# Four reorderings in a tuned convolution and SoLU kernel: transposes of y, one load of x, squares, and the last tiles' halves

## The chip, the core and the metric

The kernel runs on one core of a Trainium2 chip. The metric is the device time in microseconds (us) of one execution, from launch to end, as the median of several runs. A profile of one execution lies beside it; its span, from the first to the last instruction, is a little shorter than the time of that execution.

The engines of the core are named as the profile names them: PE (matrix multiplication; PEld is its weight load, which overlaps it), DVE, ACT and POOL (elementwise work), and SP, which here only issues transfers. Each engine works through its own list in order. All transfers of this kernel, plain ones and transposing ones, are issued by SP, one after the other, so a transfer whose data aren't ready holds up everything behind it in SP's list.

## The reference

Two layers, on x of 8 x 4160 x 192 and 33,280 tokens of 192 numbers after the first:

```python
# first: a causal convolution over 7 rows, one set of 7 softmaxed taps for each of 8 heads of 24 columns
x_unf = x_pad[:, idx, :].reshape(B, S, K, H, group)
out = np.einsum('hk,bskhg->bshg', w, x_unf)
# second: for each token
h = x @ w_in                                   # 192 -> 1024
e = np.exp(h - h_max)
solu = h * e / (np.sum(e) + 1e-09)
ln = (solu - mean) / np.sqrt(var + 1e-06) * g_ln
out = ln @ w_out                               # 1024 -> 192
```

The kernel keeps single precision by splitting numbers into a high and a low float16 half and multiplying the halves.

## The kernel before

**Chunks.** The 8 sequences are cut into 17 chunks: the first sequence into rows 0 to 1023, 1024 to 2079 and 2080 to 4159 (chunks 0, 1, 2), each of the others into two halves of 2080 rows (chunks 3 to 16). A chunk is worked in windows of 112 rows. Its x is loaded in pieces of five windows (`load`, lines 139 to 167, tile `xr`, eight buffers), scaled and split on POOL and ACT (`halve_steps`, lines 234 to 243, tile `xs`), convolved on PE group by group (`product`, line 281, result `pc` in a single PSUM bank), read out by ACT (`upper`, line 313) and DVE (`lower`, line 322) into `y16`, and transposed by SP into `yT` (`turn`, line 352). A chunk of 19 windows is turned in two parts, windows 0 to 9 and 10 to 18, each in three blocks of columns in the order 1, 0, 2. Half of block 1 is then copied to `y2` by a plain transfer (`double`, line 365). The largest value of a chunk's x, from which its scale follows, is taken by `sum_squares`: ACT squares (line 187) or DVE maxima (line 181).

**Tiles.** The second layer goes over 260 tiles of 128 tokens, numbered from 0. A tile's way is: eight matmuls of `emit_rows` (line 736, from `yT`) and two of `emit_third` (line 759) into a pair of PSUM banks `ph`; `emit_max` on DVE (line 790); `emit_exp` on ACT (797); `emit_mul` on DVE (807); `emit_hi` on ACT, the float16 upper half (815); `emit_lo` on POOL, the lower half (827), and at once its transpose into `pT` by SP (829); `emit_out` on PE, 16 or 24 matmuls (844) into a single bank `po`; `emit_evac` on DVE (854 or 852), which frees that bank. `emit_square` on ACT (819) only sums squares for the variance; its result is wanted at the end of a group of up to eight tiles, when `Group.roots` runs on POOL (912 to 916) and the rows are scaled (`row`, 921 and 925) and stored (934).

There are three pairs of banks for `ph`, so tile k+3's first matmul waits for tile k's `emit_mul`. There are two single banks, used in turn by everything that needs one: each `po`, each `pc`, the pieces of `split_taps`. The third use waits until the first has been read out.

**Order.** The schedule is written out by hand: the order of the calls in the source is the order in each engine's list. `three_steps(i)` (line 1279) emits one step of three tiles a, b, c = i, i+1, i+2, for i = 8, 11, 14 and so on. In a step PE does `emit_out` of tile i-5, the rows of a, then b, `emit_out` of i-4, the rows of c, `emit_out` of i-3, with up to four groups of convolution at the places 0 to 3 between them. `chores` (line 968) assigns to each tile of a chunk what is to be done for the chunks ahead: groups to convolve, pieces to load, to sum, to open, to turn, to double. Steps 8, 11 and 14 are marked `start` (`PAIRED` is 8). In later steps, what `chores` has to turn is put into the list `moves` at the end of the step; `move()` takes one of them, at the end of the step and after the lower halves of a and of b in the next one. The last step, tiles 257, 258 and 259, is `last_three` (line 1468).

The program below is printed with the lines of the profile.

Of the kernel before, what the change touches and what calls it, by code (L numbers as in the profile page):

```python
# [8 lines left out]
F16 = mybir.dt.float16  # L9
# [4 lines left out]
ALU = mybir.AluOpType  # L14
# [5 lines left out]
def kernel(  # L20
# [9 lines left out]
    nc = tc.nc  # L30
    P = 128
# [5 lines left out]
    NFC = F // P  # L37
    NH = F // 512
# [4 lines left out]
    FIRST = 1024  # L43
# [743 lines left out]
    def emit_max(t):  # L787

        t.bias = sp.tile([P, 1], F32, name=f"sm_{t.i}", tag="sm", bufs=4)
        dve.tensor_scalar(  # L790
            t.ph, t.ph, t.cv[:, 0:1], None, ALU.mult, ALU.min, accum_out=t.bias
        )

    def emit_exp(t):
        g, grp = t.g, t.grp
        t.e = sp.tile([P, F], F32, name=f"e_{t.i}", tag="e", bufs=4)
        act.activation(  # L797
            t.e, t.ph, AF.Exp, bias=t.bias, scale=-1.0, accum_out=grp.z[:, g : g + 1]
        )
# [17 lines left out]
    def emit_square(t):  # L817
        junk = sp.tile([P, F], F32, name=f"sq_{t.i}", tag="sq", bufs=1)
        act.activation(  # L819
            junk, t.e, AF.Square, accum_out=t.grp.s2[:, t.g : t.g + 1]  # L820
        )
        if t.g == t.grp.n - 1 and t.g:
            t.grp.squares()
            queue.put(t.grp.steps(), first=True)

    def emit_lo(t, eng):
        eng.tensor_tensor(t.p16[:, :, 1, :], t.halves, t.p16[:, :, 0, :], ALU.subtract)  # L827
        t.pT = sp.tile([P, 2 * NFC, P], F16, name=f"pT_{t.i}", tag="pT", bufs=4)
        nc.sync.dma_start_transpose(t.pT, t.p16.rearrange("p n a f -> p (n a f)"))

    def emit_out(t):
        t.po = single(f"po_{t.i}")
        t.wide = t.grp.n > 1 and t.i >= PAIRED

        ops, per = [], NFC // NH
        for c in range(NFC):
            hi = c // per * 2 * per + c % per
            if t.wide:
                ops.append((hi, ohl[:, c].rearrange("p a d -> p (a d)"), 2 * D))
            else:  # L840
                ops += [(hi, ohi[:, c], D), (hi, olo[:, c], D)]
            ops.append((hi + per, ohi[:, c], D))
        for j, (a, w, n) in enumerate(ops):
            nc.tensor.matmul(  # L844
                t.po[:, 0:n], t.pT[:, a, :], w, start=j == 0, stop=j == len(ops) - 1
            )
# [231 lines left out]
    def run_stores():  # L1078
        while stores:
            stores.pop(0)()  # L1080
# [42 lines left out]
    def numerators(t):  # L1123
        emit_mul(t)
        emit_hi(t)
# [148 lines left out]

    def loads(work):
        for c, j in work.get("load", []):
            c.load(j)

    def three_steps(i):

# [17 lines left out]
        urgent = i == PAIRED + 3  # L1298

        start = i < 2 * PAIRED  # L1300
        if not start:
            loads(work)
        got = {}
# [33 lines left out]
        def move():  # L1337

            for f in moves[:1]:
                f()  # L1340
            del moves[:1]

        def openings():
            for k in work.get("open", []):
                k.open(lefts[k.ch], chunks[k.ch - 1])
            for k, piece in work.get("turn", []):
                k.turn(*piece)

        run_stores()
        emit_out(done[0])  # L1350

# [7 lines left out]
        if start:  # L1359
            emit_max(a)  # L1360
            emit_exp(a)
            if i == PAIRED:
                for k, h in late:
                    sum_up(k, h, i - 1)
        for q in squares:
            emit_square(q)
        squares.clear()
        add(0)
        if not start:
            emit_max(a)  # L1370
# [6 lines left out]
        lowers(1)  # L1377
        emit_exp(b)
        if start:
            second()  # L1380
            if i > PAIRED:
                for k, h in late:
                    sum_up(k, h, i - 1)
                late.clear()
                uppers(2)
            for k, q in doubles:
                k.double(*q)
            doubles.clear()
        numerators(a)
        emit_lo(a, pool)  # L1390
        move()
        if i == PAIRED:
            uppers(2)
            late[:] = after
        if urgent:
            openings()
        run_stores()
# [23 lines left out]
        for d in done[2:]:  # L1421
            emit_out(d)
        place(3)
        emit_max(c)
        uppers(3)
        emit_exp(c)
# [11 lines left out]
            add(1)  # L1438
        numerators(c)
        if at(3):  # L1440
            emit_square(b)
        if PAIRED < i < 2 * PAIRED:
            add(1)
        queue.run(3.8 if i < 20 else 2.0)
        emit_lo(c, pool)
        squares.append(c)
        if urgent:
            for k, q in work["double"]:
                k.double(*q)
        elif start:  # L1450
            openings()
            doubles.extend(work.get("double", []))
        else:
            for k in work.get("open", []):
                k.open(lefts[k.ch], chunks[k.ch - 1])
            moves.extend(lambda k=k, q=q: k.turn(*q) for k, q in work.get("turn", []))
            move()
            doubles.extend(work.get("double", []))
        if i == NT - 6:
# [4 lines left out]
    def ready(t):  # L1464
        emit_z(t)
        emit_root(t)

    def last_three(i):


        a, b, c = [prepare(i + j) for j in range(3)]
        done = tiles[i - DEPTH : i]
        assert all(t.grp.n == 1 for t in (*done[3:], a, b, c))
        run_stores()
        take_rooted()
        emit_a(a, b, c, lambda: emit_out(done[0]))
        for t in (b, c):
            emit_rows(t, False, True)
        for t in squares:
            emit_square(t)  # L1480
        emit_evac(done[0])
        emit_max(a)
        emit_exp(a)
        ready(done[4])
        emit_out(done[1])
        numerators(a)
        emit_lo(a, pool)
# [67 lines left out]
```

## Time and profile before

| | before |
|---|---|
| median of 3 runs | 1171.81 us (1171.79 to 1172.24) |
| the profiled execution | 1172.57 us, of which the span is 1170.9 us |
| mean granted clock of PE | 0.995 |
| busy share of the span | PE 97%, DVE 87%, ACT 85%, POOL 75% |
| matmuls | 7742 |
| the transfer queue of SP | 225.53 MB, 99.1% of 16 transfer engines' span |
| HBM | 33.00 MB read, 25.56 MB written |

How to read it: busy shares are means over the span. The profile's list of waits gives, for an engine and a line, what it waited for, in total, how often, and the longest. A row of the timeline gives the start in us from the span's start, the duration, the engine and line, what is written and read, the number of merged instructions, and in brackets the idle time before the first of them and what ended it. A row of the stretches gives the busy time of each engine in that stretch and, after POOL's, the granted clock of PE (1.00 is full speed).

### The profile page before, as it was taken

What the parts mean: (1) busy time and instruction counts of PE and PEld (TensorE: products, weight loads), DVE (VectorE), ACT (ScalarE), POOL (GpSimd) and SP (SyncE); (2) the same over time, 40 slices, a digit from 0 to 9 for tenths busy, and PEclk for the clock granted to TensorE, in tenths of its full rate; (3) what the DMA queues carried; (4) which work ended last, traced back from release to release, by engine and by line L of the source; (5) the groups of instructions that cost most, each with busy time, mean ns of one, the idle gap of its engine ahead of it and who ended that gap; (6) DMA issues with size and microseconds to landing.
All of it is one profiled execution on the core that took longest, in us unless ns stands there. A gap on an engine that the chain in (4) does not pass through costs nothing.

```text
span 1170.9 us, 22364 instructions
## 1 busy us (share of the span) xinstructions
PE 1137.6 (97%) x7742; PEld 695.9 (59%) x7742; DVE 1017.8 (87%) x2057; ACT 997.3 (85%) x1772; POOL 878.2 (75%) x684
## 2 busy tenths in 40 slices
PE   6899998999999999999999999999999999999997
PEld 3565555666565665655656666665665666566555
DVE  8888887988989898998889989888898998788786
ACT  6998887888888898888888888888888889888885
POOL 2746778988878688887868888688788868855564
PEclk9999999999999999999999999999999999999999
DMA  8799999999999999999999999999999998999978
GB/s 224 173 185 182 179 198 201 201 194 207 188 202 208 197 190 211 216 183 204 200 199 191 208 217 184 193 208 202 202 207 199 194 193 172 173 159 196 185 150 175
DMA packets 727295, 226.95 MB, mean 194 GB/s; under 512 B 651518, under 2 KB 725774, under 8 KB 727182
## 3 DMA queue, kind: packets, MB, share of 16 engines
q1 hardware_dynamic: 727182, 225.53, 99.1%
q8 instruction: 60, 0.98, 0.3%
q14 instruction: 53, 0.43, 0.1%
HBM read 33.00 MB, written 25.56 MB: 50 GB/s over the span
## 4 chain that ended last, share of the span: by engine, by line
PE 82%; POOL 4%; DVE 4%; issue 3%; DMA 3%; ACT 3%; SPq 0%; DVEq 0%; POOLq 0%; ACTq 0%
PE po L844 37%; PE ph L736 34%; PE pc L281 5%; PE ph L759 5%; POOL p L827 2%; DMA pT<-p 2%; DVE ph L790 1%; DVE e L807 1%; ACT e L797 1%; ACT p L815 1%; DMA yT<-y 1%; POOL xs L243 1%; DMA raw_in<-in_moe_w_in_dram 1%; POOL xr L240 1%; ACT sq L819 0%
## 5 line engine op out<-in xcount | busy, mean ns | idle before, releaser
L827 POOL TENSOR_TENSOR p<-e,p 128x1024 f16<-128x1024 f32 x259 | 552.4, 2137 | 234.7 <-ACT p L815 234.4
L844 PE MATMUL po<-ohl,pT 128*128 128x192 f16 (+1 forms) x4264 | 541.6, 284 | 8.8 <-DMA pT<-p 5.3
L844 PEld LDWEIGHTS <-pT 128*128 128x128 f16 x4264 | 385.7, 98 | 168.9 <-DMA pT<-p 7.6
L736 PE MATMUL ph<-whi,yT 128*128 128x512 f16 x1548 | 420.0, 380 | 8.2 <-DMA yT<-y 5.5
L790 DVE TENSOR_SCALAR_CACHE_REDUCE ph<-ph,cv 128x1024 f32<-128x1024 f32 x248 | 318.9, 1287 | 75.0 <-PE ph L759 58.3
L797 ACT ACTIVATE e<-ph,sm 128x1024 f32<-128x1024 f32 x260 | 289.2, 1112 | 101.3 <-DVE ph L790 95.1
L807 DVE SCALAR_TENSOR_TENSOR e<-ph,cv,e 128x1024 f32<-128x1024 f32 x248 | 316.9, 1278 | 22.4 <-ACT e L797 22.2
L736 PEld LDWEIGHTS <-yT 128*128 128x128 f16 x2064 | 192.6, 98 | 237.6 <-issue 36.4
L815 ACT CAST p<-e 128x1024 f16<-128x1024 f32 x260 | 269.9, 1039 | 32.7 <-DVE e L807 32.2
L819 ACT ACTIVATE sq<-e 128x1024 f32<-128x1024 f32 x260 | 273.5, 1052 | 0.1
L736 PE MATMUL ph<-wlo,yT 128*128 128x512 f16 x516 | 153.5, 379 | 0.0
L854 DVE TENSOR_REDUCE raw<-po 128x192 f32<-128x384 f32 x247 | 136.2, 551 | 15.9 <-PE po L844 15.6
L243 POOL TENSOR_TENSOR xs<-xr,xs 128x960 f16<-128x960 f32 (+1 forms) x56 | 107.7, 1922 | 1.4
L313 ACT ACTIVATE y<-pc 112x432 f16<-112x432 f32 (+5 forms) x140 | 62.7, 469 | 17.3 <-PE pc L281 8.6
L759 PE MATMUL ph<-wlo,yT 64*128 64x512 f16 x269 | 74.0, 380 | 0.0
L281 PE MATMUL pc<-xs,taps_hi 128*112 128x240 f16 (+1 forms) x448 | 73.0, 261 | 0.0
L322 DVE SCALAR_TENSOR_TENSOR y<-pc,y 112x432 f16<-112x432 f32 (+5 forms) x140 | 72.2, 532 | 0.7 <-ACT y L313 0.7
L759 PE MATMUL ph<-wlo,y 64*128 64x512 f16 x251 | 68.6, 380 | 0.0
L181 DVE TENSOR_REDUCE xa<-xr 128x1 f32<-128x384 f32 x112 | 66.5, 616 | 2.1 <-DMA xr<-in_x_dram 2.1
L281 PEld LDWEIGHTS <-taps_hi 128*112 128x112 f16 x448 | 52.4, 130 | 16.7 <-DVE xm L203 0.3
L240 POOL TENSOR_SCALAR xr<-xr,s 128x960 f32<-128x960 f32 (+1 forms) x56 | 57.4, 1026 | 3.0
L281 PE MATMUL pc<-xs,taps_lo 128*112 128x240 f16 (+1 forms) x224 | 58.5, 261 | 0.0
(146 smaller groups left out, 785.4 us busy)
## 6 DMA issues: line engine op xcount, KB each, us to landing
out_dram<-raw SPq DMA_DIRECT2D x127, 192.0 KB, 2.9
xr<-in_x_dram SPq DMA_DIRECT2D x41, 480.0 KB, 4.8
xr<-in_x_dram SPq DMA_DIRECT2D x22, 384.0 KB, 4.1
pT<-p SPq DMA_TRANSPOSE x260, 4.6
y<-yT SPq DMA_DIRECT2D x15, 140.0 KB, 3.1
y<-yT SPq DMA_DIRECT2D x15, 126.0 KB, 2.8
yT<-y SPq DMA_TRANSPOSE x102, 3.7
raw_out<-in_moe_w_out_dram SPq DMA_DIRECT2D x1, 1536.0 KB
```

The lines of the kernel that those rows point to most:

```text
L243: (2.1 * size + 0.2, lambda: pool.tensor_tensor(xl, r, h, ALU.subtract)),
L281: nc.tensor.matmul(o, tp[:, h + j, :], r, start=q == 0, stop=q == len(ops) - 1)
L736: nc.tensor.matmul(bank, lhs, w[:, r, n * 512 : (n + 1) * 512], start=start and j == 0, stop=stop and j == len(ops) - 1,)
L759: nc.tensor.matmul(banks_of(t)[n], y[q, t.off : t.off + P], wlo[q, 1, n * 512 : (n + 1) * 512], start=start, stop=not start,)
L790: dve.tensor_scalar(t.ph, t.ph, t.cv[:, 0:1], None, ALU.mult, ALU.min, accum_out=t.bias)
L797: act.activation(t.e, t.ph, AF.Exp, bias=t.bias, scale=-1.0, accum_out=grp.z[:, g : g + 1])
L807: dve.scalar_tensor_tensor(t.e, t.ph, t.cv[:, 3:4], t.e, ALU.mult, ALU.mult, accum_out=t.grp.s1[:, t.g : t.g + 1],)
L815: act.copy(t.p16[:, :, 0, :], t.halves)
L819: act.activation(junk, t.e, AF.Square, accum_out=t.grp.s2[:, t.g : t.g + 1])
L827: eng.tensor_tensor(t.p16[:, :, 1, :], t.halves, t.p16[:, :, 0, :], ALU.subtract)
L844: nc.tensor.matmul(t.po[:, 0:n], t.pT[:, a, :], w, start=j == 0, stop=j == len(ops) - 1)
L854: dve.tensor_reduce(t.grp.raw[:, t.g, :], t.po[:, 0 : 2 * D].rearrange("p (a d) -> p d a", a=2), AX.X, ALU.add,)
```

## The change

There are six edits.

- **Turns ahead.** In the steps of tiles 17 and 26 (`soon`), the pieces of y to turn, two of them in each, go into `moves` at the start of the step, not at its end. They are so issued in that step after the lower halves of a and of b. In step 17 these are blocks 0 and 2 of chunk 2's second part, in step 26 blocks 0 and 2 of chunk 3's first part.
- **One load ahead.** `chunks[5].load(0)` is emitted in step 17 ahead of tile 19's lower half; `loads` skips it in step 20.
- **Squares behind exponentials.** In steps 8, 11 and 14 the squares left over from the step before are emitted after tile b's exponential, not ahead of it; and where a convolution stands at place 3 (steps 8 and 11), tile b's own square is left over too.
- **Step 8** emits the ACT half of a convolution's read-out (`uppers(2)`) ahead of tile 8's upper half.
- **Step 14** emits `emit_evac` of tile 11 ahead of tile 16's `emit_max`.
- **Last step.** The new `emit_halves` makes upper half, lower half and transpose in two pieces of 512 columns each. `emit_max` and `emit_exp` of b stand ahead of a's `emit_mul`, `ready` of tile 256 moves behind c's `emit_mul`.

```diff
+    def emit_halves(t, eng):
+        t.halves = t.e.rearrange("p (n f) -> p n f", n=NH)
+        t.p16 = sp.tile([P, NH, 2, 512], F16, name=f"p16_{t.i}", tag="p16", bufs=4)
+        t.pT = sp.tile([P, 2 * NFC, P], F16, name=f"pT_{t.i}", tag="pT", bufs=4)
+        for n in range(NH):
+            hi, lo = t.p16[:, n, 0, :], t.p16[:, n, 1, :]
+            act.copy(hi, t.halves[:, n])
+            eng.tensor_tensor(lo, t.halves[:, n], hi, ALU.subtract)
+            nc.sync.dma_start_transpose(
+                t.pT[:, n * NFC : (n + 1) * NFC, :],
+                t.p16[:, n].rearrange("p a f -> p (a f)"),
+            )
...
         for c, j in work.get("load", []):
-            c.load(j)
+            if c.raw[j] is None:
+                c.load(j)
...
+        soon = i in (FIRST // P * 2 + 1, FIRST // P * 3 + 2)
...
+        def root_squares():
+            for q in squares:
+                emit_square(q)
+            squares.clear()
...
+        def turns():
+            moves.extend(
+                lambda k=k, q=q: k.turn(*q) for k, q in work.get("turn", [])
+            )
...
+        if soon:
+            turns()
         run_stores()
         emit_out(done[0])
...
-        for q in squares:
-            emit_square(q)
-        squares.clear()
+        if not start:
+            root_squares()
...
         emit_exp(b)
         if start:
+            root_squares()
             second()
...
-        numerators(a)
-        emit_lo(a, pool)
-        move()
+        emit_mul(a)
         if i == PAIRED:
             uppers(2)
             late[:] = after
+        emit_hi(a)
+        emit_lo(a, pool)
+        move()
...
         place(3)
+        if fresh:
+            emit_evac(done.pop())
         emit_max(c)
...
         if at(3):
-            emit_square(b)
+            if start:
+                squares.append(b)
+            else:
+                emit_square(b)
...
+        if i == 2 * FIRST // P + 1:
+
+            chunks[5].load(0)
         emit_lo(c, pool)
...
-            for k in work.get("open", []):
-                k.open(lefts[k.ch], chunks[k.ch - 1])
-            moves.extend(lambda k=k, q=q: k.turn(*q) for k, q in work.get("turn", []))
+            opens()
+            if not soon:
+                turns()
             move()
...
         emit_exp(a)
-        ready(done[4])
-        emit_out(done[1])
-        numerators(a)
-        emit_lo(a, pool)
         emit_max(b)
         emit_exp(b)
+        emit_out(done[1])
+        emit_mul(a)
+        emit_halves(a, pool)
+        emit_mul(b)
+        emit_max(c)
         emit_out(done[2])
-        emit_max(c)
+        emit_halves(b, pool)
+        emit_exp(c)
         emit_evac(done[1])
-        emit_exp(c)
-        numerators(b)
-        emit_lo(b, pool)
         emit_evac(done[2])
         emit_out(done[3])
-        numerators(c)
+        emit_mul(c)
+        ready(done[4])
         emit_finish(done[3])
+        emit_halves(c, dve)
         for t in (a, b, c):
             emit_square(t)
-        emit_lo(c, dve)
         emit_out(done[4])
```

More of the change, by code (lines that the diff above doesn't have):

```diff
@@ L1341, in move, with opens, openings @@
             del moves[:1]
-        def openings():
+        def root_squares():
+            for q in squares:
+                emit_square(q)
+            squares.clear()
+        def opens():
             for k in work.get("open", []):
                 k.open(lefts[k.ch], chunks[k.ch - 1])
-            for k, piece in work.get("turn", []):
-                k.turn(*piece)
+        def turns():
+            moves.extend(
+                lambda k=k, q=q: k.turn(*q) for k, q in work.get("turn", [])
+            )
+        def openings():
+            opens()
+            turns()
+            while moves:
+                move()
+        if soon:
+            turns()
         run_stores()
@@ L1394, in three_steps @@
             late[:] = after
+        emit_hi(a)
+        emit_lo(a, pool)
+        move()
         if urgent:
@@ L1453, in three_steps @@
         else:
-            for k in work.get("open", []):
-                k.open(lefts[k.ch], chunks[k.ch - 1])
-            moves.extend(lambda k=k, q=q: k.turn(*q) for k, q in work.get("turn", []))
+            opens()
+            if not soon:
+                turns()
             move()
```

## The prediction

> **What bounds the kernel now.** I read the page first, then PE's list of waits.
>
> ```profile
> PE 1137.6 (97%) x7742; PEld 695.9 (59%) x7742; DVE 1017.8 (87%) x2057; ACT 997.3 (85%) x1772; POOL 878.2 (75%) x684
> ...
> PE ph L736 <- DMA yT<-y: 5.5, 2, 3.1
> PE po L844 <- DMA pT<-p: 5.3, 4, 2.0
> ...
> PE po L844 <- DVE raw L854: 2.0, 3, 1.3
> ...
> PE po L844 <- DVE y L322: 1.3, 2, 0.9
> ...
> PE pc L281 <- DVE y L322: 0.8, 1, 0.8
> ```
>
> PE works 97% of the span, and it is the engine whose idle time is the time. It waits for a transpose of y just twice, 5.5 us together; for its own transposed tiles four times, 5.3 us; and 4.1 us for DVE to free a single bank (2.0, 1.3 and 0.8). So an edit is worth what it takes out of these few places. The timeline of PE shows the two waits for yT, and the table of stretches what follows them.
>
> ```profile
> 148.24 1.89 PE L736 MATMUL ph<-whi,yT 128*128 128x512 f16 x4 [2.42 <-DMA yT<-y]
> ...
> 184.30 1.04 PE L736 MATMUL ph<-whi,yT 128*128 128x512 f16 x4 [3.10 <-DMA yT<-y]
> ```
> ```profile
> 144.77:148.18 3.41, 1.05 (x7) 0.32 (x4) 3.34 (x9) 2.21 (x4) 0.00 (x0) 1.00 1.10 150
> 148.18:151.59 3.41, 3.35 (x11) 1.64 (x12) 2.97 (x5) 3.17 (x8) 2.74 (x5) 0.50 1.12 222
> ...
> 182.31:185.72 3.41, 1.42 (x10) 0.99 (x11) 0.00 (x0) 0.88 (x2) 3.32 (x4) 1.00 1.07 222
> ```
>
> The first is the rows of tile 25, in step 23; the second those of tile 32. After the first the granted clock is 0.50 for 3.41 us, and four matmuls take 1.89 us where the same four take 1.04 at 184.30. After the second it stays 1.00. So the first wait costs 2.42 + 3.41/2 = 4.1 us, the second 3.1.
>
> **Turns ahead.** What PE waited for is in SP's list:
>
> ```profile
> 128.06 1.76 SPq L829 DMA_TRANSPOSE pT<-p  x1
> ...
> 134.66 1.85 SPq L352 DMA_TRANSPOSE yT<-y  x1
> ...
> 137.18 0.97 SPq L160 DMA_DIRECT2D xr<-in_x_dram  x2
> ...
> 138.82 4.50 SPq L829 DMA_TRANSPOSE pT<-p  x1
> 143.38 1.30 SPq L352 DMA_TRANSPOSE yT<-y  x1
> ...
> 145.54 5.87 SPq L829 DMA_TRANSPOSE pT<-p  x2
> ```
> ```profile
> 165.56 6.80 SPq L829 DMA_TRANSPOSE pT<-p  x2
> ...
> 176.39 1.37 SPq L352 DMA_TRANSPOSE yT<-y  x1
> ...
> 180.61 1.71 SPq L352 DMA_TRANSPOSE yT<-y  x1
> ```
>
> By their order, the transposes of tiles are those of 18 (128.06), 20 (138.82), 21 and 22 (145.54); 19's lies between the first two; blocks 0 and 2 of chunk 2's second part are issued at 134.66 and 143.38. With the change, block 0 goes out between tiles 17 and 18, block 2 right behind tile 18, at about 130. Only tile 18's lower half can hold it, and that one's transpose started at 128.06. Issued at 130 to 132 it lands some 10 us before tile 25's rows need it at 146. In step 26 blocks 0 and 2 move from 176.39 and 180.61 to behind tiles 26 and 27 (165.56 and the one after it, ended by 172.4): issued by 174, against a need at 181. Both waits go: **-4.1 and -3.1**.
>
> What the move adds to SP's list: 1.85 ahead of tile 18's transpose (SP idles there), 1.30 plus the load below ahead of tile 19's, 1.4 ahead of tile 27's. What stood behind them gains as much, since they leave the places ahead of tiles 20, 21, 29 and 30. PE then meets tile 20's transpose, its next need, at about 146.5. That one was issued at 138.82, a place now reached no later, and took 4.50 us because the transfers of two loads and a block lay before it.
>
> **One load ahead.** The load's two issues, some 0.5 us each (0.97 for two at 137.18), move from step 20 to just ahead of tile 19's transpose. Its buffer is long free (the reader was POOL's split of chunk 3's first piece in step 17), so it adds no wait to SP; the clearing of 16 partitions on DVE that goes with it moves too, and is small. DVE's list shows what it takes away:
>
> ```profile
> 141.74 0.55 DVE L181 TENSOR_REDUCE xa<-xr 128x1 f32<-128x384 f32 x1 [2.05 <-DMA xr<-in_x_dram]
> ```
>
> DVE idles 2.05 us for this load with tile 23's maximum behind it. PE does not wait for DVE there, so it is worth nothing by itself; but with PE 4 us earlier DVE would be late next, and these 2.05 us are its cover.
>
> [...]
>
> **Squares behind exponentials, steps 8 to 14.** The chain they are to shorten is ACT's, so I looked at where ACT idles.
>
> ```profile
> 80.68:89.09 8.41, 7.12 (x57) 5.18 (x56) 6.41 (x15) 8.38 (x19) 2.31 (x2) 1.00 1.05 220
> 105.46:115.65 10.19, 8.86 (x60) 4.68 (x58) 8.09 (x19) 10.19 (x20) 8.85 (x12) 1.00 0.95 220
> ```
> ```profile
> 91.23 0.55 DVE L854 TENSOR_REDUCE raw<-po 128x192 f32<-128x384 f32 x1
> ```
> ```profile
> 91.84 0.41 PE L844 MATMUL po<-ohl,pT 128*128 128x384 f16 x2
> ```
>
> In step 11 the squares of tiles 9 and 10 leave their places before tile 12's exponential; the three short waits of PE for `y` (1.3 + 0.8) vanish. But ACT has no gap from 80.68 to 89.09: the same work is done by the same time, the read-out of the convolution at place 2 ends where it did, and behind it in DVE's list come tile 12's `emit_mul`, tile 13's maximum and tile 8's `emit_evac` (91.23 to 91.78), for whose bank tile 9's `po` starts at 91.84. So what PE saves it waits there: 0, step 8's reordering included. In step 14 it is a loss:
>
> ```profile
> 96.05 1.05 ACT L819 ACTIVATE sq<-e 128x1024 f32<-128x1024 f32 x1
> ...
> 99.90 1.04 ACT L819 ACTIVATE sq<-e 128x1024 f32<-128x1024 f32 x1
> ...
> 100.98 1.11 ACT L797 ACTIVATE e<-ph,sm 128x1024 f32<-128x1024 f32 x1
> ...
> 105.46 1.04 ACT L815 CAST p<-e 128x1024 f16<-128x1024 f32 x1 [0.67 <-DVE e L807]
> ```
> ```profile
> 120.48 0.56 DVE L854 TENSOR_REDUCE raw<-po 128x192 f32<-128x384 f32 x1 [0.48 <-PE po L844]
> ```
> ```profile
> 121.09 2.12 PE L844 MATMUL po<-ohl,pT 128*128 128x384 f16 x16 [0.35 <-DVE raw L854]
> ```
>
> The squares of tiles 12 and 13 (96.05, 99.90) run today while ACT waits for tiles 14's and 15's maxima. Moved behind tile 15's exponential (100.98) they put 1.05 + 1.04 = 2.1 us before all that follows. The idle 0.67 at 105.46 takes up a part; ACT is 1.4 to 1.5 late from there, and from 105.46 to 115.65 it has no gap (10.19 of 10.19) to catch up in. With it DVE's list is late: it was done with tile 19's maximum at 120.0 (0.48 before 120.48) and will be at 121.5, so tile 14's `emit_evac` starts at about 121.4 instead of 120.48 (neighbours overlap by 0.1), and tile 15's `po` 0.9 later than 121.09. Tile 11's `emit_evac` ahead of tile 16's maximum takes 0.6 of the 1.3 us wait for DVE's `raw` at step 17's start; the later wait swallows it. I take **+0.9**. Bounds: +2.1, the two squares whole; -3.7, if the five waits of these steps, `y` 2.1 and `raw` 2.0 less the 0.4 of a wait far behind these steps, all went. POOL, late by the same 1.5, would delay tile 18's lower half to 129.5; block 2 stays 10 us early.
>
> **Last tiles.** Rows of DVE, SP and PE:
>
> ```profile
> 1153.17 1.27 DVE L807 SCALAR_TENSOR_TENSOR e<-ph,cv,e 128x1024 f32<-128x1024 f32 x1
> ...
> 1155.56 1.59 DVE L827 TENSOR_TENSOR p<-e,p 128x1024 f16<-128x1024 f32 x1 [0.72 <-ACT p L815]
> 1157.08 0.47 DVE L877 TENSOR_SCALAR of<-po,t,o_inv 128x192 f32<-128x192 f32 x1
> ...
> 1162.68 0.48 DVE L877 TENSOR_SCALAR e<-po,t,o_inv 128x192 f32<-128x192 f32 x1
> 1167.90 0.48 DVE L877 TENSOR_SCALAR e<-po,t,o_inv 128x192 f32<-128x192 f32 x1 [4.75 <-PE po L844]
> ```
> ```profile
> 1159.23 1.83 SPq L829 DMA_TRANSPOSE pT<-p  x1
> ```
> ```profile
> 1164.52 3.27 PE L844 MATMUL po<-ohl,pT 128*128 128x192 f16 x24 [1.95 <-DMA pT<-p]
> ```
>
> Tile 259's `emit_mul` stays at about 1153.2: b's earlier maximum and the halves of a and b before it are worth some 0.1 either way. Its lower half then has `ready` of tile 256 (about 1.0, five small instructions) and a finish (0.47) ahead, and so starts at 1155.9 and ends near 1157.5 in two pieces of half of 1.59. SP is free then: b's pieces are issued from 1153.4, not at 1156. Two pieces (1.2 to 1.3 each, the price of a block of y) are issued by 1159.2, land by about 1161.6, where 1164.5 was reached before, and the first 12 matmuls start on the first piece. PE would be done by 1162.5 at full clock. But DVE's own list, from the finish at 1157.08 to that of tile 258 at 1163.16, takes 6.1 us and now starts 0.4 later; so tile 259's finish is at 1164.1 rather than 1167.90: -3.8. With a late landing or half a clock (PE's last 24 took 3.27 us) it is -2.5. I take **-3.3**; bounds -4.0 and, if six issues of 1.26 (7.6) for three of 1.83 (5.5) stand on the path, +2.1.
>
> **Sum.** 1172.57 - 4.1 - 3.1 + 0.9 - 3.3 = 1163.0 us for the profiled execution. That one lies 0.76 above the runs' median of 1171.81, so I predict **1162.2**.
>
> **Rivals.** *The wait moves on* to tile 20's and 21's own transposes. The stretches of the transfer engines speak for it:
>
> ```profile
> 124.00:129.00 5.00, 5.00 (x34) 2.65 (x33) 4.80 (x11) 5.00 (x10) 4.92 (x3) 1.00 0.26 65
> ...
> 139.00:165.00 26.00, 23.57 (x151) 13.72 (x150) 20.91 (x47) 20.66 (x38) 14.84 (x16) 0.93 1.11 223
> ```
>
> From 139 to 165 they are full (share 1.11), and reordering a full queue frees nothing; tile 21's transpose, issued after 145.54, lands about 4.6 later (150.1) and would hold PE 1.7 us; the same at tile 27 costs another 1.4. Time 1165.3. Against it: at 124 to 129 they stand at 0.26, and block 0 moves into that hole. *The start gains*: -3.7 in place of +0.9 gives 1157.6; against it speaks ACT's full row. *The turns come late all the same*, because SP, waiting for POOL, does not reach them: 1171.81 + 0.9 - 3.3 = 1169.4, on the edge of no change; it would need 14 us of delay. *The transfer queue carries the time*, not PE: its packets took 99% of 16 engines' span. Then the 7.2 us come back as waits for pT in the steps behind, the hole before tile 18 widens by POOL's 1.5, and the last step's three added issues cost 2.1: 1171.81 + 1.5 + 2.1 = 1175.4, slower. It decides once transposes land later than PE asks for them; against it, PE waited for pT only four times in the whole span.
>
> **Chances.** The forecast 0.63 (own range 1160 to 1165), the wait moves on 0.16, the start gains 0.10, the turns late 0.05, the queue 0.06. The range 1159 to 1167 leaves out the late turns, the queue, half of the start's gain and a little of the forecast. A measurement tells about 0.2% (2.3 us) from no change: faster 0.89, same 0.05, slower 0.06.
>
> **What would show it.** No wait of PE for yT between 140 and 190, and clock 1.00 there; block 2's issue near 131; no idling of DVE for xr near 140. ACT's squares of tiles 12 and 13 between 102 and 105, and a wait of PE for `raw` of more than 1 us near 121. The last `po` starting about 6 us after the last `emit_mul` ended (before: 1164.52 - 1154.44 = 10.1). Wrong would be: waits for pT of over 1 us at tiles 20 to 28, or PE free of waits from 74 to 122.

## The result, and the profile after

The changed kernel takes 1163.40 us (median of 6 runs, 1162.06 to 1164.39), beside 1172.54 us for the kernel before in the same comparison (6 runs, 1171.79 to 1173.66): a ratio of 0.9922, with a 95% interval of 0.9909 to 0.9935. The profiled execution took 1163.45 us with a span of 1161.5, where that of before had 1172.57 and 1170.9. The forecast was 1162.2 (1159 to 1167), so the total was 1.2 us off. The terms of its sum were less good than the sum: their errors have both signs and nearly cancel, which is luck.

The page's row of the engines, and PE's list of waits (microseconds in total, times, longest):

```profile
PE 1132.2 (97%) x7742; PEld 692.4 (60%) x7742; DVE 1016.8 (88%) x2058; ACT 998.0 (86%) x1775; POOL 878.6 (76%) x686
```
```profile
PE po L859 <- DVE raw L869: 5.4, 6, 1.8
...
PE po L859 <- DMA pT<-p: 2.2, 3, 1.7
...
PE pc L281 <- DVE y L322: 0.5, 1, 0.5
```

The new functions shift later lines: `emit_out` is line 859 now (844 before), `emit_evac` 869 (854). PE's wait for yT at line 736 (5.5 us) is gone from the list (1.7 us at line 749 belong to the first tiles, near 20 us, ahead of everything that was changed); that for pT fell from 5.3 to 2.2, that for `y` at `po` and `pc` from 2.1 to 0.5. The wait for DVE to free a bank rose from 2.0 to 5.4: the profile shows at a glance that something was given back, and where.

The stretches of the changed kernel, then of the kernel before (length, busy time of PE, PEld, DVE, ACT, POOL with counts, granted clock, share of the transfer engines, GB/s):

```profile
60.00:140.00 80.00, 74.21 (x537) 47.56 (x536) 65.81 (x142) 71.85 (x138) 52.10 (x42) 1.00 0.92 180
140.00:190.00 50.00, 50.00 (x346) 30.77 (x344) 46.49 (x100) 43.08 (x77) 39.80 (x34) 1.00 1.04 207
139.00:165.00 26.00, 26.00 (x181) 16.06 (x180) 24.71 (x55) 22.64 (x42) 17.36 (x19) 1.00 1.11 219
```
```profile
60.00:140.00 80.00, 76.09 (x553) 48.95 (x552) 67.62 (x145) 71.67 (x139) 52.15 (x42) 1.00 0.91 178
140.00:190.00 50.00, 44.47 (x291) 26.06 (x288) 39.63 (x84) 38.40 (x70) 37.09 (x29) 0.97 1.06 196
```

From 140 to 190 PE is now busy in all of its 50 us, at full clock, and issues 346 matmuls where it issued 291. From 60 to 140 it is busy 1.9 us less than before: the start edits cost something. From 139 to 165, the stretch that the prediction showed, the transfer engines are as full as they were (1.11 both times), and PE doesn't wait.

To put a number on each part I use positions: when the first `po` matmul of a tile starts, in one execution less the execution of before, counted from tile 5, since executions differ by up to 2.6 us before any edit bears on PE (among the kernels here whose start is as before, tile 5's begins between 65.72 and 68.30). The starts themselves, in us:

| first `po` matmul of tile | 5 | 9 | 12 | 15 | 18 | 44 | 254 | 259 | span |
|---|---|---|---|---|---|---|---|---|---|
| before | 67.67 | 91.84 | 107.67 | 121.09 | 135.05 | 256.47 | 1149.95 | 1164.52 | 1170.85 |
| after | 67.61 | 91.97 | 108.00 | 122.87 | 137.08 | 250.90 | 1144.98 | 1155.54 | 1161.49 |

Between tiles 5 and 18 the changed kernel lost 2.1 (137.08 - 135.05 + 0.06); between 18 and 44, where both waits for yT lie, it gained 7.6; between 44 and 254 it lost 0.6; from 254 to the end it gained 4.4. Forecast were +0.9, -7.2, nothing and -3.3.

**The waits for yT.** PE's rows of tiles 25 and 32, and SP's rows of the blocks:

```profile
147.47 1.03 PE L736 MATMUL ph<-whi,yT 128*128 128x512 f16 x4
...
182.07 1.03 PE L736 MATMUL ph<-whi,yT 128*128 128x512 f16 x4
```
```profile
125.22 1.75 SPq L352 DMA_TRANSPOSE yT<-y  x1
...
130.44 1.69 SPq L829 DMA_TRANSPOSE pT<-p  x1
132.18 1.98 SPq L352 DMA_TRANSPOSE yT<-y  x1
...
167.82 1.31 SPq L352 DMA_TRANSPOSE yT<-y  x1
...
171.35 1.82 SPq L352 DMA_TRANSPOSE yT<-y  x1
```

Four matmuls take 1.03 where they took 1.89 after the first wait; no idle time stands ahead of them. The blocks are issued at 125.22 and 132.18 (134.66 and 143.38 before), at 167.82 and 171.35 (176.39 and 180.61). PE had waited for block 2 both times. The chain that ended last has it, in the kernel before, on its way until PE starts at 148.24:

```profile
143.38 4.81 DMA yT<-y
```

and again from 180.61 for 3.64 us, with PE starting at 184.30.

**The start.** DVE's and ACT's rows of step 14 in the changed kernel, the same rows of DVE before, and PE's rows after:

```profile
104.89 0.17 DVE L203 TENSOR_REDUCE xm<-pc 128x1 f32<-128x8 f32 x1 [2.58 <-ACT y L313]
...
106.19 1.27 DVE L807 SCALAR_TENSOR_TENSOR e<-ph,cv,e 128x1024 f32<-128x1024 f32 x1
...
107.39 0.55 DVE L869 TENSOR_REDUCE raw<-po 128x192 f32<-128x384 f32 x1
107.86 1.28 DVE L790 TENSOR_SCALAR_CACHE_REDUCE ph<-ph,cvm 128x1024 f32<-128x1024 f32 x1
...
118.18 1.28 DVE L807 SCALAR_TENSOR_TENSOR e<-ph,cv,e 128x1024 f32<-128x1024 f32 x1 [2.07 <-ACT e L797]
...
122.26 0.55 DVE L869 TENSOR_REDUCE raw<-po 128x192 f32<-128x384 f32 x1
```
```profile
102.84 0.17 DVE L203 TENSOR_REDUCE xm<-pc 128x1 f32<-128x8 f32 x1 [0.34 <-ACT y L313]
...
104.14 1.27 DVE L807 SCALAR_TENSOR_TENSOR e<-ph,cv,e 128x1024 f32<-128x1024 f32 x1
...
105.34 1.29 DVE L790 TENSOR_SCALAR_CACHE_REDUCE ph<-ph,cvm 128x1024 f32<-128x1024 f32 x1
...
115.77 1.28 DVE L807 SCALAR_TENSOR_TENSOR e<-ph,cv,e 128x1024 f32<-128x1024 f32 x1
```
```profile
101.92 1.05 ACT L819 ACTIVATE sq<-e 128x1024 f32<-128x1024 f32 x1
...
103.09 1.06 ACT L819 ACTIVATE sq<-e 128x1024 f32<-128x1024 f32 x1
...
104.14 0.72 ACT L313 ACTIVATE y<-pc,s 112x128 f16<-112x128 f32 x2
...
107.51 1.04 ACT L815 CAST p<-e 128x1024 f16<-128x1024 f32 x1 [0.66 <-DVE e L807]
```
```profile
91.97 2.12 PE L859 MATMUL po<-ohl,pT 128*128 128x384 f16 x16 [1.80 <-DVE raw L869]
...
108.00 2.12 PE L859 MATMUL po<-ohl,pT 128*128 128x384 f16 x16 [1.30 <-DVE raw L869]
...
120.00 2.12 PE L859 MATMUL po<-ohl,pT 128*128 128x384 f16 x16 [1.19 <-DVE raw L869]
122.87 1.30 PE L859 MATMUL po<-ohl,pT 128*128 128x384 f16 x9 [0.46 <-DVE raw L869]
```

The squares of tiles 12 and 13 (101.92, 103.09) now stand ahead of the read-out of a convolution (104.14). Behind that read-out DVE stands idle, 2.58 us instead of 0.34, so its list from line 203 on is 2.05 late (104.89 against 102.84; the executions differ by 0.06 at tile 5). Tile 11's `emit_evac` (107.39), now ahead of tile 16's maximum, adds 0.47: the maximum is 2.52 late, tile 17's `emit_mul` 2.41 (118.18 against 115.77), tile 14's `emit_evac` 1.78 (122.26 against 120.48), tile 15's `po` 1.78 (122.87 against 121.09).

**The last step.** DVE, PE and SP of the changed kernel:

```profile
1148.07 1.28 DVE L807 SCALAR_TENSOR_TENSOR e<-ph,cv,e 128x1024 f32<-128x1024 f32 x1 [0.37 <-ACT e L797]
...
1150.51 1.28 DVE L840 TENSOR_TENSOR p<-e,p 128x512 f16<-128x512 f32 x2
1151.71 0.47 DVE L892 TENSOR_SCALAR of<-po,t,o_inv 128x192 f32<-128x192 f32 x1
...
1158.14 0.48 DVE L892 TENSOR_SCALAR e<-po,t,o_inv 128x192 f32<-128x192 f32 x1 [0.38 <-PE po L859]
```
```profile
1155.54 1.16 PE L859 MATMUL po<-ohl,pT 128*128 128x192 f16 x12 [0.26 <-DMA pT<-p]
1156.86 1.16 PE L859 MATMUL po<-ohl,pT 128*128 128x192 f16 x12 [0.16 <-DMA pT<-p]
```
```profile
1146.18 5.40 SPq L841 DMA_TRANSPOSE pT<-p  x4
...
1152.30 2.61 SPq L841 DMA_TRANSPOSE pT<-p  x2
...
1158.21 0.96 SPq L893 DMA_DIRECT2D out_dram<-e  x2
```

Tile 259's two lower halves take 1.28 together (1.59 for the whole before) and are done at 1151.8; its transposes are issued by 1154.9; its `po` starts 6.2 us after the last `emit_mul` ended (1155.54 - 1149.35), where it was 10.1. Its 24 matmuls, in two portions of 1.16, run at full clock (1.00 from 1155.5 to 1158.1); before, they took 3.27, with the clock at 0.50 from 1165.35 on. Counted from tile 254, the last finish comes 4.8 earlier (1158.14 here, 1167.90 before); 0.4 of it is given back behind it, where its store is the second of two in SP's list (1158.21).

### The profile page after: what moved, and what is told of

It is laid out like the page before. It is cut to its first block, busy times and chain, and to the rows that moved or that the text cites. A ratio compares the mean times of both kernels' runs of the same rounds, so it can differ in the third digit from the quotient of the medians.

```text
span 1161.5 us, 22374 instructions
## 1 busy us (share of the span) xinstructions
PE 1132.2 (97%) x7742; PEld 692.4 (60%) x7742; DVE 1016.8 (88%) x2058; ACT 998.0 (86%) x1775; POOL 878.6 (76%) x686
## 4 chain that ended last, share of the span: by engine, by line
PE 88%; DVE 5%; ACT 2%; DMA 2%; issue 2%; POOL 1%; SPq 0%; DVEq 0%; ACTq 0%; POOLq 0%
PE po L859 40%; PE ph L736 36%; PE pc L281 6%; PE ph L759 5%; DVE e L807 1%; DMA pT<-p 1%; DVE ph L790 1%; DMA raw_in<-in_moe_w_in_dram 1%; ACT e L797 1%; ACT sq L819 0%; DVE raw L869 0%; DVE y L322 0%; POOL p L827 0%; PE mean L701 0%; DVE wlo L647 0%
## 5 line engine op out<-in xcount | busy, mean ns | idle before, releaser
L815 ACT CAST p<-e 128x1024 f16<-128x1024 f32 x257 | 266.8, 1039 | 27.9 <-DVE e L807 27.3
```

Source lines behind the costliest of these rows:

```text
L815: act.copy(t.p16[:, :, 0, :], t.halves)
```

## The experiments

Each kernel was timed beside the kernel before, whose median was 1172.61 for the first four, 1171.23 for the next four and 1172.71 for the last two. The first four do one part alone (the second, two) on the kernel before, the next three take parts out of the changed kernel, the last three split what was left. The expectations stand as written beforehand.

**1. Turns ahead, alone.** On the kernel before:

```diff
+        soon = i in (FIRST // P * 2 + 1, FIRST // P * 3 + 2)
...
+        if soon:
+            turns()
...
-            moves.extend(lambda k=k, q=q: k.turn(*q) for k, q in work.get("turn", []))
+            if not soon:
+                turns()
```

> The kernel before with the turns a step ahead alone (steps 17 and 26); load, squares, read-outs and last step as before. Theory A (each part counts on PE's list by itself, the load is only cover): both waits of PE for yT are gone, the clock stays 1.00 around 148, tile 44's first matmul comes 7.4 to 7.6 us earlier than before, the time falls by 7.0 to 7.6 us. Theory B (the parts need each other): without the load ahead DVE still idles 2 us near 141, and PE gains no more than 5 us by tile 44.

Measured: 1164.60 us against 1172.61, ratio 0.9930 (0.9914 to 0.9946). By position: -4.05 past the first wait (at tile 22's `po`, the next behind tile 25's rows), -7.32 past the second, -7.0 at tile 254. The first wait cost its 2.42 and half of the 3.41 us behind it that had run at a clock of 0.50, as forecast (4.1); the second 3.27 (forecast 3.1). Of waits for pT at tiles 20 to 28, one of 0.11 us came up, at tile 21 (146.84). Blocks 0 and 2 in the two steps, four transposes in all, are most of the change.

**2. Turns and the load.** The same kernel with one more edit:

```diff
+        if i == 2 * FIRST // P + 1:
+            chunks[5].load(0)
         emit_lo(c, pool)
```

> Turns ahead and the load ahead, nothing else. Theory A: the idling of DVE for xr near 141 is gone, PE's gain at tile 44 is that of the turns alone within 0.5 us. Theory B: at least 2 us more than the turns alone.

Measured: 1163.54 us, ratio 0.9918 (0.9903 to 0.9933); -4.08 and -7.36 by position, the same as without the load within 0.04. The load is worth nothing to PE in these executions; it does leave more room at tile 21, whose transpose landed 0.75 us before PE took it, and 0.04 before without the load. But the cover that I gave it isn't needed either. SP's and DVE's rows of the kernel with the turns alone, without the load:

```profile
134.15 0.96 SPq L160 DMA_DIRECT2D xr<-in_x_dram  x2
```
```profile
138.02 0.55 DVE L181 TENSOR_REDUCE xa<-xr 128x1 f32<-128x384 f32 x1
```

DVE's idle 2.05 us for this load is gone without moving the load: once block 0 has left its place ahead of it in SP's list, it is issued at 134.15 (137.18 before; this execution is 1.8 earlier at tile 5), and is there when DVE comes.

**3. The start edits, alone** (squares deferred in steps 8, 11 and 14, step 8's new order, tile 11's early `emit_evac`):

```diff
-        for q in squares:
-            emit_square(q)
-        squares.clear()
+        if not start:
+            root_squares()
...
         emit_exp(b)
         if start:
+            root_squares()
             second()
...
         place(3)
+        if fresh:
+            emit_evac(done.pop())
         emit_max(c)
```

> The edits of steps 8 to 14 alone: squares behind exponentials, step 8's read-out and step 14's evacuation. Theory A (squares fill idle time of ACT before, and stand in its way after): PE reaches tile 18's output matmuls 2.0 us later than before, as in the changed kernel; both yT waits stay, so part of the 2.0 may vanish in them, and the time rises by 0 to 2 us. Theory C (they are slack that PE has, or a gain): the time is unchanged or lower, and PE is no later at tile 44.

Measured: 1175.88 us, ratio 1.0024 (1.0011 to 1.0036): slower by itself. By position +1.86 at tile 15, +2.11 at tile 18, +2.49 past the first wait for yT, which grew:

```profile
150.12 1.89 PE L736 MATMUL ph<-whi,yT 128*128 128x512 f16 x4 [2.84 <-DMA yT<-y]
```

So the start edits cost the whole of my upper bound (2.1), not 0.9, and with the waits for yT still there they delay these too.

**4. The last step, alone** (`last_three` as in the changed kernel, order and halves).

> The last step's edits alone. Theory A: the time falls by 4.4 us, the whole of what the changed kernel gained between tile 254 and its end; the last output matmuls run at full clock to within the last 2.5 us. The forecast's step had 3.3. Rival: a part of it belonged to the earlier arrival at the last step, and it is 2 us or less.

Measured: 1168.06 us, ratio 0.9962 (0.9947 to 0.9977). From tile 254 to the end -4.42; in the changed kernel it was -4.39. The parts add up: with the turns at -7.3, the start at +2.1 and the last step at -4.4 the sum is -9.6, and the spans differ by 9.4; the 0.6 lost between 44 and 254 and the 0.3 by which the turns gain more in the changed kernel (7.6) lie between the two.

**5. The changed kernel without the start edits.** Steps 8 to 14 as before; the turns, the load and the last step stay.

```diff
-        if not start:
-            root_squares()
+        root_squares()
...
-        if fresh:
-            emit_evac(done.pop())
...
-            if start:
-                squares.append(b)
-            else:
-                emit_square(b)
+            emit_square(b)
```

> The changed kernel without the edits of steps 8 to 14 (squares, step 8's read-out, step 14's evacuation as before); turns, load and last step as changed. Theory A: PE reaches tile 18's output as early as the kernel before, nothing moves on, and the time is 2.0 us lower than the changed kernel's, about 1161.4. Theory C (the 2 us were slack that the turns need: with PE earlier, the wait moves on to the transposes of tiles 20 and 21): within 0.7 us of the changed kernel, with waits for pT between 140 and 160.

Measured: 1161.62 us against 1171.23, ratio 0.9915 (0.9894 to 0.9937). By position 0.00 at tile 18 and -7.35 at tile 44; PE doesn't wait at all between 140 and 186. The 2.1 us are back at tile 18 and stay to tile 44. In this execution they aren't all kept to the end: between 44 and 254 it lost 1.6 (waits for pT of 0.93 near 469 and 1.84 near 549), and in the last step it gained 3.2 instead of 4.4. That difference lies behind the last finish, where SP takes 3.53 us for four stores ahead of the last one (1.99 in the changed kernel). The total cannot be told from that of the changed kernel: the two intervals overlap.

**6. The changed kernel without step 14's squares moved** (those of tiles 12 and 13 back in their places; 9 and 10 stay deferred).

```diff
-        if not start:
+        if not start or fresh:
             root_squares()
...
-            if start:
+            if i == PAIRED:
                 squares.append(b)
```

> The changed kernel, but tile 12's square stands at the end of step 11 and tile 13's ahead of tile 15's exponential, as before; step 11's squares of tiles 9 and 10 stay behind tile 12's exponential, step 14's early evacuation stays. Theory A (the two squares of step 14 alone make the loss): DVE's 2.6 us wait for ACT near 105 goes, PE is 1.5 to 2.2 us earlier at tile 18 than in the changed kernel. Rival (the evacuation of tile 11 ahead of tile 16's maximum makes it, or the squares of step 11): less than 0.7.

Measured: 1161.42 us, ratio 0.9912 (0.9897 to 0.9927). By position -0.72 at tile 12, +0.66 at tile 15, +0.91 at tile 18, -6.69 at tile 44. So these two squares are 1.2 of the 2.1; 0.9 remain: PE is 0.72 ahead at tile 12, loses 1.38 by tile 15 and 0.25 more by tile 18. That lies between what the two theories expected.

**7. As 6, with `emit_evac` of tile 8 ahead in step 11 and none ahead in step 14.** The prediction had said that PE's gain in step 11 vanishes in the wait for this bank.

```diff
-        if fresh:
+        if i == PAIRED + 3:
             emit_evac(done.pop())
```

> As the kernel with step 14's squares in their old place, but step 14's early evacuation is undone and tile 8's evacuation in step 11 stands ahead of tile 13's maximum. Theory A: what PE saves by tile 8 (2.3 us) is no longer given back in the 1.8 us wait for that evacuation; 1 to 2 us are left at tile 10, and at tile 18, where ACT and DVE set the pace again, 0 to 1 us against the kernel before. Rival (ACT sets the pace throughout): nothing is left at tile 18, or PE is later there.

Measured: 1162.16 us, ratio 0.9917 (0.9900 to 0.9933). PE's rows of tiles 9 and 12:

```profile
91.47 2.12 PE L859 MATMUL po<-ohl,pT 128*128 128x384 f16 x16 [0.59 <-DVE raw L869]
...
107.91 2.12 PE L859 MATMUL po<-ohl,pT 128*128 128x384 f16 x16 [1.93 <-DVE raw L869]
```

The wait at tile 9 falls from 1.80 to 0.59, that at tile 12 grows from 1.3 to 1.93: of 1.02 gained at tile 9, 0.41 is left at tile 18. That is theory A, at the low end of what it had. It is the best position of all kernels at tile 44 (-7.77), and in the total no different from 5 and 6.

**8. The last step's order with whole pieces**, on the kernel before:

```diff
-        emit_halves(a, pool)
+        emit_hi(a)
+        emit_lo(a, pool)
```

and the same for b and c (from the changed kernel's `last_three`).

> The kernel before with the new order of the last step, but each tile's upper half, lower half and transpose in one piece. Theory A (the pieces make most of the 4.4 us, through a transpose that starts half a tile earlier and POOL's earlier end): from tile 254 to the end 1 to 2 us less than before. Rival (the order makes it): 3.5 us or more.

Measured: 1168.59 us, ratio 0.9972 (0.9960 to 0.9984); from tile 254 to the end -3.46. I had given the order 1 to 2, the rival 3.5 or more, and the rival has it but for 0.04: most of the last step's gain is to be had without a single half. PE's row of tile 259 (1149.95 to 1164.52 was 14.57 from tile 254's `po` before; here 12.2, from 1151.97):

```profile
1164.18 2.15 PE L859 MATMUL po<-ohl,pT 128*128 128x192 f16 x24 [0.89 <-DVE t L881]
```

**9. Tile 11's early `emit_evac`, alone**, on the kernel before:

```diff
         place(3)
+        if fresh:
+            emit_evac(done.pop())
         emit_max(c)
```

> The kernel before with one line of the change: in step 14 tile 11's emit_evac goes ahead of tile 16's maximum, and the squares stay where they are. Positions are those of each tile's first po matmul against the kernel before, counted from tile 5. What is left of the start's loss when step 14's squares are back in their places was 0.9 by tile 18. Theory A: that rest is the price of the early emit_evac: it takes 0.6 to 0.9 from PE's wait at tile 12 (near 106), but DVE then waits for PE's bank ahead of tile 16's maximum, the exponential, emit_mul and emit_max behind it come later, and tile 15's po starts 0.3 to 1.2 later; tile 18 +0.5 to +1.0. Rival: the early emit_evac is a gain that the later wait swallows (tile 12 -0.6, tile 18 within 0.3 of nothing), and the 0.9 comes from the squares of tiles 9 and 10 and from step 8's order.

Measured: 1173.91 us against 1172.71, ratio 1.0004 (0.9992 to 1.0017). By position -0.52 at tile 12, +0.47 at tile 15, +0.72 at tile 18: theory A, though PE saved 0.52 at tile 12 and not 0.6 to 0.9. The total can't be told from that of the kernel before. DVE's and PE's rows:

```profile
104.92 0.56 DVE L869 TENSOR_REDUCE raw<-po 128x192 f32<-128x384 f32 x1 [0.66 <-PE po L859]
105.39 1.28 DVE L790 TENSOR_SCALAR_CACHE_REDUCE ph<-ph,cvm 128x1024 f32<-128x1024 f32 x1
```
```profile
105.98 2.13 PE L859 MATMUL po<-ohl,pT 128*128 128x384 f16 x16 [0.81 <-DMA pT<-p]
...
120.39 2.12 PE L859 MATMUL po<-ohl,pT 128*128 128x384 f16 x16 [0.46 <-DVE raw L869]
```

PE's wait at tile 12 is 0.8 instead of 1.3. But DVE, which had no idle time there, now stands 0.66 us waiting for tile 11's matmuls, with tile 16's maximum behind. That maximum is 1.2 late (105.39, in an execution that is 1.17 ahead at tile 5, against 105.34), and tile 15's `po` pays. One wait of PE was exchanged for one of DVE, which cost more. Experiment 7 agrees from the other side: with the squares of 9 and 10 and step 8's order as changed, and tile 11's `emit_evac` in its old place, PE is ahead at tile 18.

**10. The last step's halves in the old order**, on the kernel before:

```diff
-        numerators(b)
-        emit_lo(b, pool)
+        emit_mul(b)
+        emit_halves(b, pool)
```

and so for a and c, each in its old place.

> The kernel before with the last step's halves alone: each tile's upper half, lower half and transpose in two pieces, in the old order of the list. Counted is the time from tile 254's po to the span's end against the kernel before. The whole last step gave -4.4 there, its new order with whole pieces -3.5. Theory A: the two add up, order -3.5 and halves -0.9 (-0.4 to -1.5), tile 259's po starting on the first piece 1 to 1.5 earlier. Rival B: the halves need the order (tile 259's lower half goes to DVE as late as before, and six issues take 7.6 on the queue instead of 5.5): 0 to +1.5. Rival C: the two are ways to the same gain: -2 to -3.5 each by itself.

Measured: 1169.74 us against 1172.71, ratio 0.9977 (0.9959 to 0.9995); from tile 254 to the end -3.23. PE's rows of tile 259:

```profile
1162.10 1.17 PE L859 MATMUL po<-ohl,pT 128*128 128x192 f16 x12 [0.90 <-DVE raw L940]
1164.01 1.16 PE L859 MATMUL po<-ohl,pT 128*128 128x192 f16 x12 [0.75 <-DMA pT<-p]
```

Order -3.5, halves -3.2, both -4.4: rival C. They are two ways to the same gain, and do not add up. The ends alone don't say how much more the two give together: both gave 4.4 in three executions, but 3.2 and 3.0 in experiments 5 and 7, and the old step takes 0.6 to 0.8 longer in experiments 1, 2, 3 and 9 than in the execution of before. The last finish, ahead of SP's stores, is steadier. After tile 254's `po` it comes at 17.95 in the kernel before (18.5 to 18.7 in those four), at 14.5 with the order or the halves alone, and at 13.0 to 13.2 in all five kernels with both. In both, and in the whole step, tile 259's matmuls take 2.15 for 24, or twice 1.16, the latter in the changed kernel at a granted clock of 1.00; before, they took 3.27, at 0.50 from 1165.35 on: 1.1 us of each is that.

## Why the prediction was right or wrong

**Turns ahead: right**, in place, mechanism and size: -4.33 and -3.27 in the changed kernel against -4.1 and -3.1. Block 2 was issued at 132.18 rather than near 131, because tile 18's transpose, which it stands behind, came 2.4 later (130.44 against 128.06) and not 1.5: the same underestimate of the start. There was room; PE asked at 147.5. "The wait moves on" fell: the list of waits has pT three times in the whole span, the longest 1.73, and at 550, not at tiles 20 to 28. The argument that reordering a full queue frees nothing fails because it matters which transfer lands when: from 139 to 165 the engines are as full as before, but block 2, which PE had waited for, goes out at 132.18, ahead of that stretch, and block 0 at 125.22, in the hole (share 0.26 there before, 0.95 now). It was close, though: tile 21's transpose landed at 150.18, as that rival had it (150.1), and PE, 2.1 late from the start edits, took it at 150.41. In the five kernels with the turns that reach tile 18 earlier (experiments 1, 2, 5, 6 and 7) it landed 0.04 to 0.75 us before PE took it.

**The load: worth 0 as predicted, for another reason.** I kept it as the cover for DVE's 2.05 us. With the turns alone, that idle time is gone as well (experiment 2): moving the blocks also moves what stands behind them.

**Start edits: the sign right, the size wrong** (+0.9 forecast, +2.1 measured, at the upper bound). Two steps of the working failed.

- "The idle 0.67 at 105.46 takes up a part; ACT is 1.4 to 1.5 late from there". That idle time ends with `emit_mul` of tile 15 on DVE, and this `emit_mul` stands in DVE's list behind its half of the convolution's read-out, whose ACT half stands behind the two squares. The delay came round through DVE: `emit_mul` was 2.05 late, and ACT still idles 0.66 at 107.51. Slack that ends with work which is itself late is no slack. Experiment 6 gives the two squares 1.2 of the 2.1.
- "Tile 11's `emit_evac` ahead of tile 16's maximum takes 0.6 of the 1.3 us wait for DVE's `raw` at step 17's start; the later wait swallows it." It was costed on PE's side alone. Experiment 9 has the 0.5 on PE, and then 0.7 lost at tile 18, because tile 16's maximum stands behind an `emit_evac` that waits for PE. I named what PE waits for and not what is queued behind the moved instruction on DVE. In the changed kernel, where DVE is late anyway, the wait is gone but 0.47 of the reduction itself stays in front of the maximum. Taken out of the changed kernel, the two squares are worth 1.2; the early `emit_evac` alone costs 0.7; all the start edits together cost 2.1.

That PE's savings in step 11 would vanish was right: PE's waits for `y` in steps 8 and 11 fell from 2.1 to 0.5, tile 9's wait for its bank came up with 1.80, tile 9 starts 0.2 later than before. The wait near 122 that I named (over 1 us) is split in two: 1.19 at 120.00 and 0.46 at 122.87.

**Last step: right in mechanism, short by 1.1** (-3.3 forecast, -4.4 measured). The limit of the working was DVE's list, 6.1 us from tile 256's finish to tile 258's; it took 6.05 (1151.71 to 1157.76). Four sizes were off. Tile 259's lower half began 1.2 us after the last `emit_mul` ended, not 1.5 (1150.51 - 1149.35, against 1155.9 - 1154.44), and its "two pieces of half of 1.59" were 1.28 together: the list began 0.7 earlier than I had it. The sum set the end of tile 259's finish (1164.1) against the start of that of before (1167.90); start against start its own figures give -4.3, not -3.8. And I took -3.3 for the chance of a late landing or half a clock: no half clock came (the granted clock is 1.00 from 1155 on), and a late landing cost 0.4, since the transposes were issued 5.6 us after the last `emit_mul` ended, not 4.8, and DVE, done with its list, idled 0.38 for PE. Another 0.4 went behind the last finish, at the stores. Order and halves I had not told apart: experiments 8 and 10 show that either gives 3.2 to 3.5 by itself.

**What I did not forecast:** 0.6 us between tiles 44 and 254. A wait for pT of 1.73 us near 550 stands for most of it, where before it was 1.08 near 555. PE waits 1.1 to 2.1 us at that place in every other kernel too, between 546 and 558. Why its size varies isn't settled: between kernels whose lists are the same there, the time over this stretch differs by as much as 1.6 us (from +0.05 in experiment 7 to +1.62 in 5), so I put no part of it down to the change.

**The total** was 1.2 above the forecast: +1.2 at the start, +0.6 between 44 and 254, -1.1 in the last step and -0.4 at the waits add up to +0.3 against the sum for the profiled execution (1163.0, measured 1163.45; 0.2 of the rest lies outside the span). That these errors cancel is luck, not a good sum. The other 0.7 is the median: I took off the 0.76 us by which the profiled execution of before stood over the median of three runs. After, the profiled execution stands 0.05 over its median, and six runs of before have theirs at 1172.54.

**Left open:** whether a version without the start edits beats the changed one. Experiments 5 to 7 stand at 0.9912 to 0.9917 and the change at 0.9922; by position they are 1.2 to 2.3 better at tile 44, but the intervals, of 0.15% to either side and more, hold all four.

## What to carry to other kernels

An idle gap absorbs a delay only if the work that ends it isn't downstream of that delay: follow the releaser of the gap back through the other engine's list before you count on it. When a small instruction is moved ahead to end one engine's wait, read what stands behind it on its own engine, and whether it will have to wait there itself; in experiment 9, 0.5 us for PE cost 1.2 us for DVE. The cheapest edits were in the list of transfers: four transposes of y, two in each of two steps, moved past a few others gave 7 of the 9 us, and took along the loads behind them.

## What the runs showed of the hardware

The length of a wait of PE did not settle whether half a clock followed it. In the kernel before, the granted clock was 0.50 from 35.54 to 38.95 and from 148.18 to 151.59, 3.41 us each time, and again from 1165.35 to the end of the span. Between these lie 109.23 us (38.95 to 148.18) and 1013.76 us (151.59 to 1165.35). An estimate from these times: 109.23 us are 32 stretches of 3.41, and a 32nd of it goes 297.0 times into 1013.76, so the changes of the clock in this execution fit stretches of one length that follow each other without a shift. In the kernel of experiment 9, PE waited 2.97 us until 148.13 (longer than the 2.42 of before, which was followed by half a clock), and its next four matmuls took 1.04, just as four did at 184.30 in the kernel before, at a clock of 1.00. After its second wait, 3.08 us until 183.87, four took 1.59. The granted clock is 1.00 up to 184.20, and I put its fall there, an estimate. Stretches of this length, counted back from there:

```profile
143.24:146.66 3.42, 1.92 (x15) 1.11 (x12) 3.32 (x10) 2.22 (x5) 0.00 (x0) 1.00 1.14 162
146.66:150.07 3.41, 1.94 (x13) 1.22 (x14) 3.18 (x8) 2.74 (x6) 2.36 (x3) 1.00 1.02 219
180.79:184.20 3.41, 0.33 (x3) 0.21 (x3) 1.03 (x3) 1.40 (x2) 3.32 (x3) 1.00 1.07 217
```

By this count the first wait was split over two of them, each with PE busy for 1.9 of 3.41 us, and the second fell into a single one (0.33 busy). So where a wait falls may count as well; two waits don't settle it. That the clock stayed up after the first wait saved nothing here: PE waited another 1.17 us for tile 21's transpose at 152.29, and from tile 18's `po` to tile 22's it took 24.53 us, against 24.48 before. Nor did the busy time of a stretch settle what followed. In the kernel before, half a clock followed stretches with PE busy for 1.05 us (144.77), 1.46 (1161.94) and 1.65 (32.13), and none followed one with 1.42 (182.31). What decides isn't shown.

Transposes of half a tile were not half as dear to SP: in the changed kernel four took 5.40 us and two 2.61, 1.3 each, and in experiment 10 four took 6.38, beside 1.83 for tile 259's whole one before. And the same instruction on DVE, the whole lower half of tile 259, took 1.59 us before and 1.22 in the kernel of experiment 8:

```profile
1157.49 1.22 DVE L827 TENSOR_TENSOR p<-e,p 128x1024 f16<-128x1024 f32 x1
```

In the kernel before, POOL's last lower half was still running when DVE began (until 1156.07, against 1155.56). In the changed kernel POOL was done by 1149.24, DVE began at 1150.51, and its two halves took 0.68 each, 1.28 together. In experiment 10 the two halves took 1.80 together. Whether POOL's work is the cause wasn't tried.
